# A fused attention and maxout kernel on one core: loads placed where GpSimd has no mark to set, one z loaded a step ahead, PSUM pairs given out by PE's own times

## The chip, the cores and the metric

The kernel runs on one core of a Trainium2 chip. The core has five engines that take part here: TensorE (PE in the profile; PEld is its weight load, which runs beside the matmuls), VectorE (DVE), ScalarE (ACT), GpSimd (POOL) and SyncE (SP). SP does nothing but issue DMAs; POOL issues DMAs too and sets small marks. Two DMA queues carry nearly all data: q0, filled by POOL, and q1, filled by SP. The metric is the device time of one execution in microseconds, lower is better.

## The reference

There are eight sequences of 3072 tokens. For each, attention without a softmax is computed from z (64 wide) and v (256 wide), and gated with u (256 wide). A maxout MLP with 1024 hidden units follows on every token.

```python
# u, v: (8, 3072, 256); z: (8, 3072, 64); w1, w2: (256, 1024); w_out: (1024, 256)
scores = (1.0 / 3072) * np.matmul(z, z.transpose(0, 2, 1))
attn = np.maximum(scores, 0.0) ** 2
x = (u * np.matmul(attn, v)).reshape(8 * 3072, 256)
h1, h2 = x @ w1, x @ w2
out = np.maximum(h1, h2) @ w_out
```

All data come and go as float32; the products are made in bfloat16 with float32 sums in PSUM.

## The kernel before

**Tiles and steps.** The work is cut into 48 steps, n = 6b + s: step s of sequence b makes the outputs of 512 tokens (a group: G = 4 blocks of 128; NG = 6 groups a sequence). In the steady state a step takes about 18.5 us, a sequence 111.2 us. Each step has these stages, and the MLP of a step runs three steps later (LAG = 3), between the products of the later step:

- scores: z zᵀ for pairs of blocks, from zT, the transposed z of the sequence (`score`, L260). ACT or DVE apply the relu and the square (`relu`, `square`) and give a tile `a_sb`. Since the scores are symmetric, blocks that are needed in the other orientation are turned by DMA transposes on SP (`turn`).
- attention products: (attn v)ᵀ. The first three steps (PLAIN) do it plainly. Later steps use a Winograd form of Strassen's method with seven products in place of eight. It needs sums of blocks: DVE makes S1 to S4 from the attention tiles for each step and group, and folds v once for each sequence (`add_fold`, tile `lf`, from the six v tiles of the sequence in pairs of two). On PE the products are four lists a step: Xa, Xb, Ya, Yb, each going over the six groups.
- gating: DVE makes xT from the product in PSUM (`acc`) and uT (L296). uT is u, turned by one DMA transpose on SP.
- MLP: max(h1, h2) is h2 plus the relu of h1 − h2. So d jobs (L1109) multiply x with w1 − w2, ACT or DVE apply the relu and give `g_sb`, and o jobs (L1188) multiply `g_sb` with w_out and x with w2 w_out, which is made once (`W2o_sb`). Copies to `o_sb` and a store by SP follow.

**Half rows and marks.** PE works with 64 of its 128 rows at a time, two matmuls side by side, each for a different PSUM bank (`halved`, L99). Both halves of a sum go into the same bank, and so the second half may begin only when the first is through. That is said by a mark: GpSimd sets one column of `mark_sb` when the newest matmul of the first half is done (`mark`, L94 to 97; the memset is L95), and the first matmul of the second half waits for this memset (`fence`, in `matmul`, L86 to 92). Xb waits so for Xa, Yb's first product for Ya's first, the last Ya for Yb; the d and o jobs have marks of their own (L700 to 705, `halves_of`, `parts`). There are 364 marks in all.

**Loads.** u (256 KB a step), v (six of 256 KB a sequence) and z (384 KB a sequence) are loaded by POOL with `load` (L107, L108). A timed load waits for the newest matmul issued at its place in the program. POOL works in its program's order, so a mark that comes behind a load waits for it, and the other way round. z of every sequence from 1 on goes into the same tile, `z_sb_0`; then SP turns it with two transposes into zT (`make_zT`, L117 to 121), which has two buffers.

**What sets the order.** PE's order is written out by hand (`work`, L1267 on) and becomes the list `pe_order`, with planned starts `pe_at` and a planned start of each step, `starts`. `at_step(b, s, us)` (L1472) gives the first PE job planned at or after `us` microseconds into step s of sequence b. `add_u` (L1478), `add_z` (L1506) and `add_v` (L343) take such a job as the place of their load. Before, u of the next step is loaded 4 us into a step (2 us in sequence 0), z of sequence b at (step 2, 9 us) of sequence b − 1, and at (step 3, 8 us) for sequence 1; its turn is at (3, 12), for sequence 1 at (3, 18).

The orders of ACT, DVE, SP and POOL come from a planner that runs while the program is built: `link` (L1680) draws up who depends on whom, `find_dues` (L1715) gives each job the time at which it is wanted, from `plan`, which adds up PE's costs (L1710), and `find_orders` (L1739) plays the jobs through with planned costs, with `settle` (L1754) for the DMAs. This is repeated for 24 rounds, and the round with the earliest end of PE is kept. PSUM has three pairs of banks for scores and MLP (`mm`); `share_mm` (L1833) gives each user one of them: of the pairs free in PE's order, that which comes free first. Before, it took the time when a pair comes free from the planner's `done`, and it was done again at rounds 2, 4 and 6 (`PAIRS_AT`, L195).

SEVEN (L54), the steps whose output products would use a seven-product form (`add_seven`, L923), is an empty tuple in both kernels.

Of the kernel before, what the change touches and what calls it, by code (L numbers as in the profile page):

```python
# [11 lines left out]
def kernel(  # L12
# [27 lines left out]
    P = 128  # L40
# [142 lines left out]
    ALONE, XB_TO, YA_FROM, YA_FIRST, O_CLEAR = 4, 2, 2, 6, 2  # L183


    PE128, PE256, PE512, SWITCH = 56, 109, 216, 100
    TT = {256: 205, 512: 336, 1024: 603, 1536: 870}
    RELU = {"ACT": 912, "DVE": 1140}
    RELU_LAST = {"ACT": 264, "DVE": 345}
# [2 lines left out]
    LAST_BLOCKS = 60  # L192
    COPY_O = {"ACT": 470, "DVE": 610}
    PATIENCE, WAIT_COST = 400, 20
    ROUNDS, PAIRS_AT = 24, (2, 4, 6)  # L195
    RELU_BIAS, SQUARE_BIAS = 1200, -300
    TURN, TURN_LAG, UT_LAG = 1750, 4000, 7000

# [32 lines left out]
    def tile_of(pool, key):  # L231
        return bufs[pool, key].tile
# [52 lines left out]
    def copy(eng, out_ap, in_ap):  # L285
        pin(nc.scalar.copy(out_ap, in_ap) if eng == "ACT" else nc.vector.tensor_copy(out_ap, in_ap))  # L286
# [609 lines left out]
    def w_half(k, c):  # L896
        return w_out_sb[:, ds(k * KF // 2, KF // 2), ts(c, P)]
# [25 lines left out]
    def add_seven(st):  # L923
# [5 lines left out]
        def R(k, t):  # L929
            return tile_of(*gk)[:, ds(k * KF // 2, KF // 2), ts(t, HW)]  # L930

        def made(i):
            return tile_of(*sk)[:, i]

        halves = [("g", n, 0), ("g", n, 1)], [("g", n, 2), ("g", n, 3)]
        for name, fn, deps in (
# [12 lines left out]
                lag=180,  # L949
            )  # L950

        half_m = range(KF // 2)

        def at_ps(at, j):
            bank, pos, tile_i = at
            return tile_of("mm", ("o", n, tile_i))[:, bank, ds(pos * HW + j * P, P)]

        def run(at, moving_w, x):
            return [(at_ps(at, j), x[:, m, ts(j, P)], moving_w[:, m, :]) for m in half_m for j in range(2)]

        def x_part(at, h, c):
            return [
                (at_ps(at, j), tile_of(*xT)[:, h, dc, ts(j, P)], W2o_sb[:, dc, ts(c, P)])
                for dc in range(KD)
                for j in range(2)
            ]

        def bank_lists():
            return {
                "a": run((0, 0, 0), w_half(0, 0), R(0, 0)) + x_part((0, 1, 0), 0, 0) + run((0, 1, 0), w_half(1, 0), R(1, 0)),
                "b": x_part((1, 0, 0), 1, 0) + x_part((1, 1, 0), 1, 1) + run((1, 0, 0), wf_sb[:, 3], R(1, 1)),
                "c": run((0, 0, 1), wf_sb[:, 2], made(0)) + run((0, 1, 1), wf_sb[:, 1], made(1)),
                "d": run((1, 0, 1), wf_sb[:, 0], R(0, 1)) + x_part((1, 1, 1), 0, 1) + run((1, 1, 1), w_half(1, 1), made(2)),
            }

        def slots(first, end):
            lists = bank_lists()  # L980
            sides = [[(name, i) for name in names for i in range(len(lists[name]))] for names in ("adbc", "bcad")]
            for at in range(first, end):
                for half in range(2):
                    name, i = sides[half][at]
                    second = ("adbc".index(name) > 1) != (half == 1)
                    if second and i == 0:
                        fence.append(marks.pop((n, name)))
                    end_of = i == len(lists[name]) - 1
                    halved(half, *lists[name][i], start=not second and i == 0, stop=second and end_of)
                    if not second and end_of:  # L990
                        marks[n, name] = mark()

        P0, P1 = ("mm", ("o", n, 0)), ("mm", ("o", n, 1))
        base = [("w2o", 0), ("w2o", 1)] + [("wf", i) for i in range(4)]
        firsts = halves[0] + halves[1][:1] + base
        for i, (first, end, deps, new, uses) in enumerate(
            (
                (0, 14, firsts, [P0, P1], [gk, xT]),
                (14, 20, halves[1] + [("G3", n)], None, [gk, xT, sk]),
                (20, 24, [("G1", n)], None, [gk, sk]),  # L1000
                (24, 32, [("G2", n)], None, [gk, xT, sk]),
                (32, 56, [("G4", n)], None, [gk, sk, xT, P0, P1]),
                (56, 72, [], None, [sk, xT, gk, P1]),
            )
        ):
            job(
                ("o", n, i),
                {"PE": (end - first) * PE128},
                lambda _, first=first, end=end: slots(first, end),
                deps=deps,  # L1010
                new=new,
                uses=uses,
                lag=150,
            )

        def ps(i, bank, pos=None):
            t = tile_of("mm", ("o", n, i))[:, bank, :]
# [11 lines left out]
        def right():  # L1029
            return tile_of(*ok).rearrange("p (h j) (c d) -> p h j c d", h=2, c=2)[:, :, :, 1, :]  # L1030

        for name, ways, fn, deps, uses in (
            ("oc0", {"ACT": 270}, lambda e: copy("ACT", C(0, 1), two(ps(0, 0, 0))), [("o", n, 4)], [P0]),
            (
                "oc1",
                {"ACT": 470},
                lambda e: copy("ACT", low(), ps(0, 1).rearrange("p (c j d) -> p c j d", c=2, j=2)),
                [("o", n, 4)],
                [P0],
            ),  # L1040
            ("oA", {"DVE": 336}, lambda e: add(C(0, 0), C(0, 1), two(ps(0, 0, 1))), [("oc0", n)], [P0]),
            ("oB", {"DVE": 336}, lambda e: add(C(0, 1), C(0, 1), two(ps(1, 0, 1))), [("oA", n), ("o", n, 5)], [P1]),
            ("oC", {"DVE": 336}, lambda e: add(two(tile_of(*tk)), C(0, 1), two(ps(1, 0, 0))), [("oB", n)], [P1, tk]),
            ("oD", {"DVE": 603}, lambda e: add(right(), right(), twice(ps(1, 1, 0))), [("oC", n), ("oc1", n)], [P1]),
            ("oE", {"DVE": 336}, lambda e: add(C(0, 1), C(0, 1), two(ps(1, 1, 1))), [("oD", n)], [P1]),
            ("oF", {"DVE": 603}, lambda e: add(low(), low(), twice(tile_of(*tk))), [("oD", n)], [tk]),
        ):
            job(
                (name, n),
                ways,  # L1050
                fn,
                deps=deps,
                new={"oc0": ok, "oC": tk}.get(name),
                uses=[ok] + uses,
                after=[("oc0", n)] if name == "oc1" else (),
                lag=200,
            )
# [221 lines left out]

    def put_o(n, per=2):  # L1280
        if n >= 0 and steps[n].seven:
            for i, count in enumerate((14, 6, 4, 8, 24, 16)):
                put(count * PE128, True, ("o", n, i))
        elif n == last:
            for i in range(G):
                put(1090, True, ("o", n, i))
        elif n >= 0:
            for i, count in enumerate((20, 10, 10)):
                put(count * PE256, True, ("o", n, i))
# [182 lines left out]
    def at_step(b, s, us):  # L1472
        return pe_job_at(starts[NG * b + s] + us * 1000)

    def z_deps(st):
        return [("zT", st.b)] if st.b else []

# [44 lines left out]
    for n in range(len(steps)):  # L1522
        b, s = steps[n].b, steps[n].s
        if n == 0:
            add_u(0, None)
        else:
            pb, ps = divmod(n - 1, NG)
            add_u(n, at_step(pb, ps, 2 if pb == 0 else 4))
    for b in range(1, B):
        if b == 1:  # L1530
            z_at, zT_at = (3, 8), (3, 18)
            v_at = [(4, 8), (4, 13), (4, 17.5), (5, 2), (5, 8), (5, 11)]
        else:
            z_at, zT_at = (2, 9), (3, 12)
            v_at = [(3, 8), (3, 14), (4, 5), (4, 12), (5, 2), (5, 6)]
        add_z(b, at_step(b - 1, *z_at), at_step(b - 1, *zT_at))
        for g, at in zip(v_order(b), v_at):
            add_v(b, g, at_step(b - 1, *at))

    W2, W2T = ("T", "w2"), ("T", "w2T")  # L1540
    bufs[W2] = Buf(lambda tag: widepool.tile([P, KD, Dff], bf16, name="w2_sb", tag=tag))
# [288 lines left out]
        return uses  # L1830


    def share_mm():  # L1833
        def end(key):
            return max([j.done for j in bufs["mm", key].jobs] + [0])

        keys = order["mm"]
        uses = [[], [("mm", keys[0]), ("mm", keys[2])], [("mm", keys[1]), ("mm", keys[3])]]
        free_at = [0, end(keys[2]), end(keys[3])]
        for key, slot in zip(keys, (1, 2, 1, 2)):  # L1840
            bufs["mm", key].slot = slot
        last_use = [-1] * 3
        for key in keys[4:]:
            at = position[taker["mm", key].key]
            slot = min([i for i in range(3) if last_use[i] < at], key=lambda i: free_at[i])
            last_use[slot] = max(position.get(j.key, -1) for j in bufs["mm", key].jobs)
            free_at[slot] = end(key)
            uses[slot].append(("mm", key))
            bufs["mm", key].slot = slot
        return uses  # L1850
# [5 lines left out]
    find_orders()  # L1856
    wide = share_wide()
    pairs = share_mm()
    for turn_no in range(ROUNDS):
        if turn_no in PAIRS_AT:  # L1860
            pairs = share_mm()
        link(wide + pairs)
        find_dues()
        found = find_orders()
# [99 lines left out]
```

## Time and profile before

| | us |
|---|---|
| median of 3 runs | 922.25 (921.33 to 922.66) |
| profiled execution: its own time | 919.85 |
| its span in the trace (granted clock 0.998) | 917.8 |
| PE busy | 904.8 (99%) |
| DVE, ACT, POOL busy | 692.4 (75%), 652.7 (71%), 95.4 (10%) |
| share of 16 DMA engines: q1 (SP), q0 (POOL) | 75.8%, 23.2% |
| u load, v load, z load, issue to landing (medians) | 5.6, 5.7, 6.7 |
| uT transpose, issue to landing (median) | 5.8 |

The span is the time from the first to the last instruction of the profiled execution; 2.05 us of its own time lie around it. "Landing" is the time when the data of a DMA are there, counted from its issue. In rows of the timeline the first number is the start in us, the second the duration, then engine, line, operation and tiles; a bracket at the end gives how long the engine had been idle and what it waited for. A row of the waits reads: engine, its line, who released it; total, number of times, longest. A matmul of 64 rows by 256 columns runs beside that of the other half, and such pairs start every 109 to 110 ns; those with 512 columns every 212 to 216.

### The profile page before, as it was taken

Reading aid. Unit: us, or ns where it says so; the run is one execution under the profiler, and the core shown is the slowest. Engines: PE = TensorE matmul, PEld = TensorE weight load, DVE = VectorE, ACT = ScalarE, POOL = GpSimd, SP = SyncE. Lnnn points to the kernel's source line nnn. Section 1 sums busy time; section 2 is a strip of 40 time slices with the busy share of each in tenths; the row PEclk is TensorE's granted clock in tenths of the full one; section 3 lists DMA queues with packets and bytes.
Section 4 is the critical chain, followed back from the end, with each engine's and each line's share of the span. In section 5 each row is a group of like instructions: output and inputs, shape, how many; then the busy total and the mean of one; then the engine's idle time right before and its main releaser. Section 6 shows DMA issues by size and latency. Waiting matters only on the chain.

```text
span 917.8 us, 31948 instructions
## 1 busy us (share of the span) xinstructions
PE 904.8 (99%) x13813; PEld 668.6 (73%) x13813; DVE 692.4 (75%) x1356; ACT 652.7 (71%) x780; POOL 95.4 (10%) x479
## 2 busy tenths in 40 slices
PE   9998999999999999999999999999999999999998
PEld 3366777777777777777777777778777777777775
DVE  6766788768886888778886788778878777888641
ACT  8865887568766778667786587865888558874534
POOL 2100100111001110011100110001100011000000
PEclk9999999999999999999999999999999999999999
DMA  9999999999999999999999999999999999997711
GB/s 162 122 186 199 177 192 180 161 180 146 172 161 172 182 151 152 172 169 170 152 174 176 156 162 167 166 174 173 161 158 171 145 192 160 168 160 136 115 36 70
DMA packets 382909, 146.32 MB, mean 159 GB/s; under 512 B 361264, under 2 KB 362928, under 8 KB 382768
## 3 DMA queue, kind: packets, MB, share of 16 engines
q1 hardware_dynamic: 366208, 114.54, 75.8%
q0 software_dynamic: 16560, 29.74, 23.2%
q8 instruction: 108, 1.77, 0.8%
q14 instruction: 33, 0.27, 0.1%
HBM read 59.77 MB, written 25.17 MB: 93 GB/s over the span
## 4 chain that ended last, share of the span: by engine, by line
PE 94%; DMA 2%; ACT 2%; issue 1%; POOL 1%; DVE 0%; SPq 0%; POOLq 0%; DVEq 0%
PE acc L87 47%; PE s_ps L87 47%; ACT a_sb L275 1%; DMA uT<-u_sb 1%; DMA zT<-z_sb 1%; ACT a_held L275 0%; POOL z_sb L108 0%; DMA o_sb<-in_z_dram 0%; SPq L104 0%; POOL mark_sb L95 0%; DVE xT L296 0%; ACT a_sb L281 0%; PE tpz L130 0%; DVE a_sb L283 0%; DVE zT L131 0%
## 5 line engine op out<-in xcount | busy, mean ns | idle before, releaser
L87 PEld LDWEIGHTS <-v_sb 64*128 64x128 bf16 (+1 forms) x4464 | 313.5, 94 | 81.4 <-POOL mark_sb L95 16.8
L275 ACT ACTIVATE a_sb<-s_ps 128x1024 bf16<-128x1024 f32 x337 | 302.0, 942 | 62.1 <-PE s_ps L87 59.1
L87 PEld LDWEIGHTS <-lf 64*128 64x128 bf16 x3240 | 251.9, 94 | 45.9 <-POOL mark_sb L95 15.9
L87 PE MATMUL acc<-es,v_sb 64*128 64x256 bf16 x2160 | 277.4, 269 | 0.0
L283 DVE TENSOR_TENSOR a_sb<-a_sb 128x1024 bf16<-128x1024 bf16 (+1 forms) x240 | 149.7, 637 | 145.2 <-ACT a_sb L275 138.7
L87 PE MATMUL acc<-es,lf 64*128 64x256 bf16 x1080 | 247.7, 269 | 0.1
L87 PE MATMUL acc<-a_sb,lf 64*128 64x256 bf16 x1224 | 227.0, 269 | 0.0
L275 ACT ACTIVATE g_sb<-s_ps 128x1024 bf16<-128x1024 f32 x187 | 186.3, 1025 | 13.4 <-PE s_ps L87 12.7
L87 PE MATMUL s_ps<-w_out_sb,g_sb 64*128 64x256 bf16 x3008 | 194.9, 269 | 0.0
L87 PE MATMUL s_ps<-xT,w_sb 64*128 64x512 bf16 (+1 forms) x1484 | 189.8, 377 | 2.9 <-POOL mark_sb L95 2.8
L87 PE MATMUL acc<-aT,lf 64*128 64x256 bf16 x936 | 174.4, 270 | 0.0
L87 PEld LDWEIGHTS <-g_sb 64*128 64x128 bf16 x3008 | 146.3, 94 | 18.2 <-issue 0.4
L286 ACT COPY o_sb<-s_ps 128x512 f32<-128x512 f32 (+1 forms) x98 | 56.5, 577 | 136.7 <-PE s_ps L87 136.7
L289 DVE TENSOR_TENSOR e<-e,acc 128x512 f32<-128x512 f32 (+1 forms) x225 | 126.2, 577 | 29.4 <-ACT e L286 16.2
L87 PE MATMUL acc<-a_sb,v_sb 64*128 64x256 bf16 (+1 forms) x1352 | 140.9, 281 | 1.3 <-POOL mark_sb L95 1.3
L87 PEld LDWEIGHTS <-w_sb 64*128 64x128 bf16 (+1 forms) x1488 | 68.0, 94 | 74.5 <-POOL mark_sb L95 33.7
L87 PE MATMUL s_ps<-zT 64*128 64x512 bf16 (+2 forms) x774 | 115.9, 335 | 3.6 <-DMA zT<-z_sb 3.3
L289 DVE TENSOR_TENSOR es<-aT 128x1536 bf16<-128x1536 bf16 (+1 forms) x117 | 106.6, 930 | 0.2
L95 POOL MEMSET mark_sb<- 128x1 bf16 x364 | 37.1, 102 | 616.6 <-PE s_ps L87 440.5
L281 ACT ACTIVATE a_sb<-a_sb 128x1024 bf16<-128x1024 bf16 (+1 forms) x98 | 93.1, 969 | 1.2
L292 DVE TENSOR_TENSOR es<-a_sb 128x512 bf16<-128x512 bf16 x198 | 80.3, 418 | 15.2 <-PE acc L87 14.7
L87 PE MATMUL acc<-aT,v_sb 64*128 64x256 bf16 x936 | 85.8, 271 | 0.2 <-DVE xT L296 0.2
(58 smaller groups left out, 557.2 us busy)
## 6 DMA issues: line engine op xcount, KB each, us to landing
out_dram<-o_sb SPq DMA_DIRECT2D x47, 512.0 KB, 4.6
v_sb<-in_v_dram POOLq DMA_DIRECT2D x48, 256.0 KB, 5.7
u_sb<-in_u_dram POOLq DMA_DIRECT2D x48, 256.0 KB, 5.6
aT<-a_sb SPq DMA_TRANSPOSE x230, 4.9
z_sb<-in_z_dram POOLq DMA_DIRECT2D x7, 384.0 KB, 6.7
w_sb<-in_moe_w_dram POOLq DMA_DIRECT2D x2, 512.0 KB, 10.9
uT<-u_sb SPq DMA_TRANSPOSE x48, 5.8
a_sb<-a_sb SPq DMA_TRANSPOSE x45, 4.4
```

Source lines behind the costliest of these rows:

```text
L87: newest[0] = pin(nc.tensor.matmul(*args, **kw)).ins
L95: ins = pin(nc.gpsimd.memset(mark_sb, 0.0)).ins
L275: pin(nc.scalar.activation(out_ap, in_ap, AF.Relu))
L281: pin(nc.scalar.activation(ap, ap, AF.Square))
L283: pin(nc.vector.tensor_mul(ap, ap, ap))
L286: pin(nc.scalar.copy(out_ap, in_ap) if eng == "ACT" else nc.vector.tensor_copy(out_ap, in_ap))
L289: pin(nc.vector.tensor_add(*args))
L292: pin(nc.vector.tensor_sub(*args))
```

## The change

It has four parts.

1. A function `quiet` is added. A place planned from the start of step 3 (LAG) on moves on to the next job of a fixed set: the first group's Xb, Ya or Yb of a step. It is applied to all timed loads of u, z and v, not to those of the weights.
2. z of sequence 1 is loaded at (step 2, 6 us) in place of (3, 8), and turned at (3, 2) in place of (3, 18).
3. `share_mm` gives the pairs out once, and takes the time at which a pair comes free from PE's plan: the planned start of the pair's last PE job, that job's PE time, and a constant for the reads behind it (1200 ns; 900 for outputs).
4. `add_seven` is written anew with three PE jobs in place of six, and the constants and `put_o` with it. With SEVEN empty it is not called.

```diff
-    ROUNDS, PAIRS_AT = 24, (2, 4, 6)
+    ROUNDS = 24
+    READ_O, READ_PLAIN = (1500, 3000), (900, 900)
...
+    QUIET = {("Xb", n, st.groups[0]) for n, st in enumerate(steps)} | {
+        (part, n, st.groups[i]) for n, st in enumerate(steps) for part, i in (("Ya", 0), ("Yb", 0))
+    }
+
+    def quiet(at):
+        i = pe_order.index(at[0])
+        if pe_at[i] < starts[LAG]:
+            return at
+        found = [key for key in pe_order[i:] if key in QUIET]
+        return found[:1] or at
...
-            add_u(n, at_step(pb, ps, 2 if pb == 0 else 4))
+            add_u(n, quiet(at_step(pb, ps, 2 if pb == 0 else 4)))
     for b in range(1, B):
         if b == 1:
-            z_at, zT_at = (3, 8), (3, 18)
+            z_at, zT_at = (2, 6), (3, 2)
             v_at = [(4, 8), (4, 13), (4, 17.5), (5, 2), (5, 8), (5, 11)]
...
-        add_z(b, at_step(b - 1, *z_at), at_step(b - 1, *zT_at))
+        add_z(b, quiet(at_step(b - 1, *z_at)), at_step(b - 1, *zT_at))
         for g, at in zip(v_order(b), v_at):
-            add_v(b, g, at_step(b - 1, *at))
+            add_v(b, g, quiet(at_step(b - 1, *at)))
...
     def share_mm():
-        def end(key):
-            return max([j.done for j in bufs["mm", key].jobs] + [0])
-
         keys = order["mm"]
...
-        free_at = [0, end(keys[2]), end(keys[3])]
+        free_at, last_use = [0, 0, 1], [-1] * 3
...
             last_use[slot] = max(position.get(j.key, -1) for j in bufs["mm", key].jobs)
-            free_at[slot] = end(key)
+            user = pe_order[last_use[slot]]
+            reads = 1200
+            if key[0] == "o":
+                reads = (READ_O if steps[key[1]].seven else READ_PLAIN)[key[2] % 2]
+            free_at[slot] = plan[user] + jobs[user].ways["PE"] + reads
...
-    for turn_no in range(ROUNDS):
-        if turn_no in PAIRS_AT:
-            pairs = share_mm()
+    for _ in range(ROUNDS):
         link(wide + pairs)
```

More of the change, by code (lines that the diff above doesn't have):

```diff
@@ L183 @@
     ALONE, XB_TO, YA_FROM, YA_FIRST, O_CLEAR = 4, 2, 2, 6, 2
-    PE128, PE256, PE512, SWITCH = 56, 109, 216, 100
+    PE128, PE256, PE512, SWITCH, CHANGE = 56, 109, 216, 100, 150
     TT = {256: 205, 512: 336, 1024: 603, 1536: 870}
@@ L952, in add_seven, with run @@
         half_m = range(KF // 2)
+        def run(todo, ends=False):
+            for at, moving_w, x in todo:
+                for m in half_m:
+                    for j in range(2):
+                        first = (m, j) == (0, 0) and at[1] == 0
+                        last = (m, j) == (KF // 2 - 1, 1) and ends
+                        matmul(
+                            at_ps(at, j),
+                            x[:, m, ts(j, P)],
+                            moving_w[:, m, :],
+                            start=first,
+                            stop=last,
+                        )
@@ L954, in at_ps @@
         def at_ps(at, j):
-            bank, pos, tile_i = at
+            tile_i, bank, pos = at[2], at[0], at[1]
             return tile_of("mm", ("o", n, tile_i))[:, bank, ds(pos * HW + j * P, P)]
[L958 to L966, printed above, removed]
@@ L971, in bank_lists @@
[L971 to L977, printed above, removed]
@@ L979, in slots @@
[L979 to L991, printed above, removed]
@@ L993, in add_seven, with x_part, first @@
-        P0, P1 = ("mm", ("o", n, 0)), ("mm", ("o", n, 1))
+        def x_part(at, h, c, last):
+            for dc in range(KD):
+                for j in range(2):
+                    matmul(
+                        at_ps(at, j),
+                        tile_of(*xT)[:, h, dc, ts(j, P)],
+                        W2o_sb[:, dc, ts(c, P)],
+                        start=False,
+                        stop=last and dc == KD - 1 and j == 1,
+                    )
+        def first(_):
+            run([((0, 0, 0), w_half(0, 0), R(0, 0)), ((0, 1, 0), w_half(1, 0), R(1, 0))])
+            x_part((0, 1, 0), 0, 0, True)
+            run([((1, 0, 0), wf_sb[:, 3], R(1, 1))])
+            x_part((1, 0, 0), 1, 0, False)
+            x_part((1, 1, 0), 1, 1, True)
@@ L994, in add_seven, with second, third @@
+        def second(_):
+            run([((0, 0, 1), wf_sb[:, 2], made(0)), ((1, 0, 1), wf_sb[:, 0], R(0, 1))])
+        def third(_):
+            run([((0, 1, 1), wf_sb[:, 1], made(1))], ends=True)
+            run([((1, 1, 1), w_half(1, 1), made(2))])
+            x_part((1, 1, 1), 0, 1, True)
         base = [("w2o", 0), ("w2o", 1)] + [("wf", i) for i in range(4)]
-        firsts = halves[0] + halves[1][:1] + base
-        for i, (first, end, deps, new, uses) in enumerate(
-            (
[L998 to L1003, printed above, removed]
-            )
-        ):
[L1006 to L1014, printed above, removed]
+        for i, (fn, ns, deps, new, uses) in enumerate(
+            (
+                (first, 36 * PE128 + CHANGE, halves[0] + halves[1] + base, ("mm", ("o", n, 0)), [gk, xT]),
+                (second, 16 * PE128, [("G3", n), ("G1", n)], ("mm", ("o", n, 1)), [gk, sk]),
+                (third, 20 * PE128, [("G2", n), ("G4", n)], None, [sk, xT, ("mm", ("o", n, 1))]),
+            )
+        ):
+            job(("o", n, i), {"PE": ns}, fn, deps=deps, new=new, uses=uses, lag=150)
@@ L1030, in right @@
             return tile_of(*ok).rearrange("p (h j) (c d) -> p h j c d", h=2, c=2)[:, :, :, 1, :]
+        P0, P1 = ("mm", ("o", n, 0)), ("mm", ("o", n, 1))
         for name, ways, fn, deps, uses in (
-            ("oc0", {"ACT": 270}, lambda e: copy("ACT", C(0, 1), two(ps(0, 0, 0))), [("o", n, 4)], [P0]),
+            ("oc0", {"ACT": 270}, lambda e: copy("ACT", C(0, 1), two(ps(0, 0, 0))), [("o", n, 0)], [P0]),
             (
@@ L1037, in add_seven @@
                 lambda e: copy("ACT", low(), ps(0, 1).rearrange("p (c j d) -> p c j d", c=2, j=2)),
-                [("o", n, 4)],
+                [("o", n, 0)],
                 [P0],
@@ L1041, in add_seven @@
             ("oA", {"DVE": 336}, lambda e: add(C(0, 0), C(0, 1), two(ps(0, 0, 1))), [("oc0", n)], [P0]),
-            ("oB", {"DVE": 336}, lambda e: add(C(0, 1), C(0, 1), two(ps(1, 0, 1))), [("oA", n), ("o", n, 5)], [P1]),
+            ("oB", {"DVE": 336}, lambda e: add(C(0, 1), C(0, 1), two(ps(1, 0, 1))), [("oA", n), ("o", n, 2)], [P1]),
             ("oC", {"DVE": 336}, lambda e: add(two(tile_of(*tk)), C(0, 1), two(ps(1, 0, 0))), [("oB", n)], [P1, tk]),
@@ L1281, in put_o @@
         if n >= 0 and steps[n].seven:
-            for i, count in enumerate((14, 6, 4, 8, 24, 16)):
-                put(count * PE128, True, ("o", n, i))
+            put(36 * PE128 + CHANGE, True, ("o", n, 0))
+            put(16 * PE128, True, ("o", n, 1))
+            put(20 * PE128, True, ("o", n, 2))
         elif n == last:
@@ L1833, in share_mm @@
     def share_mm():
-        def end(key):
-            return max([j.done for j in bufs["mm", key].jobs] + [0])
         keys = order["mm"]
         uses = [[], [("mm", keys[0]), ("mm", keys[2])], [("mm", keys[1]), ("mm", keys[3])]]
-        free_at = [0, end(keys[2]), end(keys[3])]
+        free_at, last_use = [0, 0, 1], [-1] * 3
         for key, slot in zip(keys, (1, 2, 1, 2)):
             bufs["mm", key].slot = slot
-        last_use = [-1] * 3
         for key in keys[4:]:
```

## The prediction

> **What bounds the kernel now.** The busy shares come first: PE is busy 904.8 of 917.8 us (99%), DVE 75%, ACT 71%, POOL 10%. So PE sets the end, and only what makes PE idle or slow can be won. The view of waits says what PE stood still for:
>
> ```profile
> PEld L87 <- POOL mark_sb L95: 66.4, 178, 1.8
> ...
> PEld L87 <- DMA zT<-z_sb: 3.6, 1, 3.6
> PE s_ps L87 <- DMA zT<-z_sb: 3.3, 1, 3.3
> ...
> PE s_ps L87 <- POOL mark_sb L95: 2.8, 6, 0.5
> ...
> PE acc L87 <- POOL mark_sb L95: 1.3, 1, 1.3
> ```
>
> The columns are us in total, times, longest. PEld's 66.4 is no loss, since weight loads run beside matmuls. PE's own rows are: zT once, six waits on a mark in s_ps, one in acc. Next, the timeline at each. One of the six:
>
> ```profile
> 164.35 0.10 POOL L95 MEMSET mark_sb<- 128x1 bf16 x1 [2.75 <-PE s_ps L87]
> ...
> 164.86 0.53 POOL L108 DMA_DIRECT2D z_sb<-in_z_dram  x1 [0.41 <-PE s_ps L87]
> ...
> 165.38 0.12 POOL L95 MEMSET mark_sb<- 128x1 bf16 x1
> ...
> 165.55 1.04 PE L87 MATMUL s_ps<-xT,w_sb 64*128 64x512 bf16 x8 [0.45 <-POOL mark_sb L95]
> ```
>
> The load of z holds POOL for 0.53 us, the mark stands behind it, and PE waits for the mark. The matmuls start at 164.73 and 165.55, 0.82 apart where 0.21 is usual: 0.61 lost. It recurs at 276.76, 387.97, 499.18, 610.39 and 721.89 (0.608 to 0.635). The acc row is a load of u:
>
> ```profile
> 847.74 0.54 POOL L108 DMA_DIRECT2D u_sb<-in_u_dram  x1 [4.98 <-PE s_ps L87]
> 848.27 0.28 POOL L95 MEMSET mark_sb<- 128x1 bf16 x2
> ...
> 848.44 0.39 PE L87 MATMUL acc<-a_sb,v_sb 64*128 64x256 bf16 x4 [1.34 <-POOL mark_sb L95]
> ```
>
> This load began 2.70 us after the matmul it waits for, all others 0.31; its mark came 1.50 us late. Last, the wait for zT of sequence 1, and the windows with the granted clock (second number: PE busy; after POOL's: PEclk):
>
> ```profile
> 84.12 0.39 PE L87 MATMUL s_ps<-zT 64*128 64x256 bf16 x4 [3.30 <-DMA zT<-z_sb]
> ```
> ```profile
> 82.10:85.50 3.40, 1.38 (x20) 0.94 (x22) 1.85 (x4) 0.95 (x1) 0.20 (x2) 0.98 1.22 238
> 85.50:88.90 3.40, 3.40 (x38) 2.46 (x34) 0.69 (x1) 2.05 (x3) 0.00 (x1) 0.52 1.19 199
> ```
>
> PE waits from 80.66 to 84.12 (3.46), then runs a window at clock 0.52, which costs 3.40 x 0.48 = 1.63; by the spacing of the matmuls it is 1.65.
>
> **The change, part by part.** PE's own list of matmuls is the same in both programs; the loads' places, the orders of SP and ACT, DVE's order up to about 130 us, and the PSUM pairs differ.
>
> (a) z of sequence 1, earlier. z goes out at 62.52, lands at 68.00, and SP issues its two zT transposes at 75.06 to 79.33, landing at 84.07. After the change the load waits for the matmul at 46.27, and SP has the transposes ahead of its entries of about 67: at 4.3 us of issue and 4.7 more to land they are there by 77 at the latest, ahead of 80.66. The wait goes, and the slow window with it: −3.46 −1.65 = **−5.1**. What is late next: the inputs that DVE makes for PE stand over 2 us ahead in this stage. On POOL nothing is queued behind the load until 54; u of step 4 takes its old place at 63.7, 2 us ahead of the next mark (65.81), and its turn at 68.87 goes behind zT without harm, since uT stands some 20 us ahead of its xT from here on.
>
> (b) z of sequences 2 to 7 moves from 164.86 to 167.31 (and alike), where the next mark is 0.9 us or more away: 6 x 0.61 = **−3.7**. Its zT is still turned by SP's place in step 3; zT stood 0.18 to 1.69 us ahead of its first score, and SP's new order has it one entry ahead of uT in most sequences, some 1.5 us more. So nothing is late there.
>
> (c) The u load of 847.74 moves to 849.23, behind that mark: **−1.5**.
>
> (d) The other moved loads of u and v. Here a new risk: the u load in step 5 of seven sequences (108.19, 219.38 ... 775.7) ends 0.03 us ahead of the next mark PE needs. In before six v loads have 0.04, and none made PE wait; such a mark costs nothing when free. Two marks (665.37, 781.68) were 0.29 late with no load ahead; whether these go or three come is open: 0, from −0.6 to +0.3.
>
> (e) What z's new place costs. At 46.27 the queues are full: w_out (40.84) and u (41.76) are being read, and SP has issued uT of step 2 at 43.56 to 45.84. While GpSimd's loads (q0) are served, transposes (q1) nearly stand; only after 50.4 do they run:
>
> ```profile
> q0 software_dynamic: 1023, 0.67, 128.2%
> q1 hardware_dynamic: 169, 0.04, 8.5%
> ```
> ```profile
> q1 hardware_dynamic: 4224, 1.05, 128.6%
> ```
>
> The first is 46.5 to 50.0, the second 50.5 to 55.0. uT lands at 52.58, and DVE's xT waits for it already:
>
> ```profile
> 52.67 0.69 DVE L296 SCALAR_TENSOR_TENSOR xT<-acc,uT 128x512 bf16<-128x512 f32 x1 [3.09 <-DMA uT<-u_sb]
> ```
>
> PE then loses 0.39 at 54.62. z's packets began 1.1 us after its issue at the old place (62.52, 63.6); from 47.4 it stands behind u in q0, ahead of the moment (50.4) at which q1 is let in. Its 0.39 MB take 2.1 us at the first row's 0.67 MB in 3.5; at the old place they took up to 3.8 (63.6 to 67.4). I take 2.2, nearest to the crowded row: uT lands at 54.8. DVE's new order puts a square ahead of xT, which would let PE go at 54.02 + 2.2 = 56.2 against 54.23 wanted: 2.0 lost, against 0.39 now: **+1.6** (−0.4 with uT untouched, +3.2 with 3.8).
>
> Does that wait bring a slow window? The nearest row is the 1.50 us stand at 848: the window behind it is at 1.00. The 3.46 stand had one. I take 0, bound +1.7. [...]
>
> (f) DVE's new order in steps 3 to 7: a fold for sequence 1 ends at about 123.3 where its product is wanted at 123.04: **+0.2** (0 to 0.4).
>
> (g) PSUM pairs: almost everywhere pairs 0 and 1 change names; one score at 47.45 waits 0.1 for a relu, within the wait of (e). 0. The rewritten seven-product output is never built (SEVEN is empty): 0.
>
> Sum: −5.1 −3.7 −1.5 +0 +1.6 +0.2 = −8.5. The profiled execution's 919.85 (span 917.8 and 2.05 around it) becomes 911.35. It stands 2.40 below the median of the runs, so I forecast 922.25 − 8.5 = **913.8**.
>
> **The rivals.**
> 1. The same with a slow window behind the wait at 54: +1.65, up to +1.6 more if z takes 3.8: 915.4 to 917.0. For it: 2.0 us lies between a stand without (1.50) and one with (3.46).
> 2. z is served behind uT 2, and delays only the turns that follow. Then the 0.39 goes, and a product at 58.2 waits about 0.9: +0.5 in place of +1.6: 912.7. For it: uT was issued 2.7 us earlier. Against: q1 at 8.5% while q0 is served.
> 3. Marks are still late at the new places: the seven u loads with 0.03 us of room. At the 0.29 of the late marks seen: 7 x 0.3 = +2.1: 915.9. Against: six loads with 0.04 did no harm.
> 4. Slower. The last v loads of sequences 2 to 7 go out later (218.39 for 217.47), behind them u. DVE runs without a gap for 10.9 us from the fold of these v (227.87) to the sums PE wants, with 0.3 to spare. The fold starts 9.5 us after the load is issued in the new program, so a load that lands L us after issue costs L − 9.8 each. At L = 11.8 it is 2.0 x 6 = 12: 925.8. It ends above 924.1 from L = 11.5 on (1.72 x 6 = 10.3). Seen for this load: 7.13 to 10.41; the 10.41 would cost 0.6. Against: second loads of a pair, as u and v are here, landed after 6.27 to 8.37. For it: a load has been late, by 2.4 us, at 847.74. [...]
> 5. The change does not do what it says: zT still late since SP does not reach it, or z is held. Then (a) is lost: 922.25 − 3.4 = 918.9. At 68.87 to 72.3 SP was busy with others' transposes, but zT's order is fixed ahead of them.
>
> **How the numbers follow.** Forecast 0.45; rival 1 0.20; rival 2 0.14; rival 3 0.08; rival 4 0.08; rival 5 0.05. What this kernel's measurement can tell from no change is about 0.2%, 1.84 us: faster is below 920.4, slower above 924.1. Rivals 1, 2, 3 and 5 end faster, with 0.05 of all these near enough to 920.4 to count as the same: faster 0.87, same 0.05, slower 0.08. The range goes from 911.0 (913.8 less the 2.0 to the lower end of (e), the 0.6 of (d) and the 0.2 of (f)) to 918.0 (plus 1.65 for a slow window, 1.6 for z at 3.8, 0.3 of (d), 0.2 of (f): 917.6, rounded up). It leaves out rivals 4 and 5, 0.13.
>
> **What would show it.** In the profile after: no wait of PE for zT; no row of PE s_ps on a mark with 0.5, none of 1.3 in acc; no clock of 0.5 at 85. A wait of DVE for uT near 50 to 55 of 5 us instead of 3.09, and a PE gap of some 2 us at 54 to 56: (e). A slow window behind it is rival 1. Gaps at 108, 219 and on of 0.3 are rival 3; PE waiting on sums about 235, 346 is rival 4. The forecast is wrong if DVE, not the loads, holds PE in steps 2 to 4, where its order changes most, or if a later place of u or v delays what I followed only by before's times.

## The result, and the profile after

The changed kernel takes 913.67 us (median of 9 runs, 910.70 to 917.57), the kernel before 921.33 (9 runs, 917.08 to 923.31). The ratio is 0.993, with a 95% interval of 0.9907 to 0.9952. The forecast was 913.8. Medians here and below are of all runs of a kernel, while the ratios leave out three runs that took over 1.5% longer than the fastest of their kernel. The profiled execution took 915.26, its span is 913.3; the profiled execution of the kernel before took 919.85, 4.6 more.

The rows of PE (and one of DVE) among the waits of the changed kernel; columns as before:

```profile
DVE lf L290 <- DMA v_sb<-in_v_dram: 3.3, 1, 3.3
...
PE acc L87 <- DVE lf L290: 2.7, 1, 2.7
...
PE s_ps L87 <- POOL mark_sb L95: 0.5, 2, 0.3
PE acc L87 <- DMA v_sb<-in_v_dram: 0.5, 1, 0.5
```

PE no longer waits for zT, of its waits for marks 0.5 us is left, and there is a new wait: DVE for a v, and PE for the fold that DVE makes of it. The next rows show the timeline where z of sequence 2 is loaded, and where the load of u stood ahead of a mark near 848:

```profile
165.19 0.10 POOL L95 MEMSET mark_sb<- 128x1 bf16 x1 [0.33 <-PE s_ps L87]
...
166.51 0.10 POOL L95 MEMSET mark_sb<- 128x1 bf16 x1 [1.22 <-PE s_ps L87]
...
167.13 0.53 POOL L108 DMA_DIRECT2D z_sb<-in_z_dram  x1 [0.51 <-PE acc L87]
```
```profile
846.50 0.54 POOL L108 DMA_DIRECT2D u_sb<-in_u_dram  x1 [2.90 <-PE s_ps L87]
847.03 0.28 POOL L95 MEMSET mark_sb<- 128x1 bf16 x2
...
847.20 1.04 PE L87 MATMUL s_ps<-xT,w_sb 64*128 64x512 bf16 x8 [0.32 <-POOL mark_sb L95]
```

The marks come first now and z behind them. The load of u is still ahead of a mark, but of one that is wanted later: PE loses 0.48 instead of 1.50.

PE's order is the same in all kernels here, so one matmul can be followed through every trace. From the start of the 1751st matmul (152.59 us before, 153.00 after) to the end of the span, the kernel before takes 765.20 us, the changed one 760.33. So 4.9 us are won behind 150 us, and the first part, where z's new place should have won 5.1, took 0.4 us longer; together they are the 4.5 us between the spans. The starts of the same matmuls split the 0.4: 4.85 are won near 80 to 90 (the wait for zT and the slow window behind it) and 0.5 near 55; 5.2 are lost between 115 and 131, and 0.55 in the first 10 us, ahead of every load that was moved. That beginning alone differs by some 2 us between the traces of this document. Between 115 and 131 PE stood here; the last two rows are windows with their length, the busy time of PE, PEld, DVE, ACT and POOL, and then the granted clock:

```profile
118.89 0.39 PE L87 MATMUL acc<-a_sb,v_sb 64*128 64x256 bf16 x4 [0.46 <-DMA v_sb<-in_v_dram]
122.02 0.28 PE L87 MATMUL acc<-a_sb,lf 64*128 64x256 bf16 x2 [2.73 <-DVE lf L290]
```
```profile
118.80:122.20 3.40, 0.58 (x8) 0.29 (x10) 0.67 (x2) 0.41 (x1) 0.00 (x0) 1.00 1.30 108
122.20:125.60 3.40, 3.40 (x30) 1.90 (x28) 3.40 (x10) 2.49 (x3) 0.73 (x3) 0.53 1.06 222
```

The v in question was issued at 107.37 and landed 14.1 us later. PE was busy 0.58 us of the first window, and the next one ran at clock 0.53, which costs 3.40 x 0.47 = 1.6.

### The profile page after: what moved, and what is told of

Its sections match the earlier page's. It is cut to its first block, busy times and chain, and to the rows that moved or that the text cites. A ratio compares the mean times of both kernels' runs of the same rounds, so it can differ in the third digit from the quotient of the medians.

```text
span 913.3 us, 31984 instructions
## 1 busy us (share of the span) xinstructions
PE 903.4 (99%) x13813; PEld 667.9 (73%) x13813; DVE 693.3 (76%) x1357; ACT 651.1 (71%) x779; POOL 95.4 (10%) x479
## 4 chain that ended last, share of the span: by engine, by line
PE 96%; DMA 2%; ACT 1%; POOL 0%; issue 0%; DVE 0%; POOLq 0%; DVEq 0%
PE s_ps L87 48%; PE acc L87 48%; DMA v_sb<-in_v_dram 2%; ACT a_sb L276 1%; DMA z_sb<-in_z_dram 1%; ACT a_held L276 0%; PE tpz_c L130 0%; DVE lf L290 0%; POOL u_sb L108 0%; ACT o_sb L287 0%; POOL mark_sb L95 0%; POOL ident masks.py:199 0%; POOL ident masks.py:197 0%; POOL z_sb L174 0%; POOL z_sb L175 0%
## 5 line engine op out<-in xcount | busy, mean ns | idle before, releaser
L276 ACT ACTIVATE a_sb<-s_ps 128x1024 bf16<-128x1024 f32 x337 | 301.9, 942 | 58.2 <-PE s_ps L87 55.9
L87 PEld LDWEIGHTS <-lf 64*128 64x128 bf16 x3240 | 251.8, 94 | 48.6 <-POOL mark_sb L95 15.6
L276 ACT ACTIVATE g_sb<-s_ps 128x1024 bf16<-128x1024 f32 x187 | 185.7, 1025 | 13.7 <-PE s_ps L87 13.3
```

Of the source, the lines that this page charges most:

```text
L87: newest[0] = pin(nc.tensor.matmul(*args, **kw)).ins
L276: pin(nc.scalar.activation(out_ap, in_ap, AF.Relu))
```

## The experiments

My theory was that the parts add up and that the late v was chance of the DMA queues. The rivals were that it belongs to the new order, and that the first part is bound by the amount of DMA work. "First part" below is the time to the 1751st matmul, "rest" what follows. What PE lost at a wait is the distance of two matmul starts beyond the usual one. The runs of one group were made on one chip, beside the kernel before; the second and third group on the same chip.

**First group** (before: 921.4). The changed kernel again; no edit.

> The changed kernel once more, for a second trace and more spans with their clocks. Theory (late v is chance of the DMA queues): the 2.9 us wait of VectorE for a v of sequence 1 near 119 to 122, and the slow window behind it, are in some executions only: spans fall into two groups, about 909 (granted clock 1.000) and 912 to 916 (0.996 to 0.998), and the new trace has either no wait there or one of another length. Rival (the wait belongs to the new order of loads): the second trace has it again at 2.5 us or more, and the spans at clock 1.000 need another cause.

914.1 us, ratio 0.9917 (0.9889 to 0.9945). v took 11.6 us to land in place of 14.1, PE lost 1.10 there and 1.36 at two turns near 102. The wait has another length: it goes with the execution. The two groups of times did not show: the runs at a granted clock of 0.999 to 1.000 took 912.1 to 915.3. The rest is 760.35.

z's place alone:

```diff
-            z_at, zT_at = (3, 8), (3, 18)
+            z_at, zT_at = (2, 6), (3, 2)
```

> The kernel before with z of sequence 1 loaded at (step 2, 6 us) and turned at (3, 2), nothing else. Theory (parts add up): the wait for zT (3.46 us) and the slow window behind it (1.65) go, the six waits of 0.6 and the one of 1.5 at 848 stay: about 5.1 us less than before, ratio 0.9945, and no clock of 0.5 near 85. If the late v of sequence 1 comes with z's new place: 2 to 4 us of it are given back at 119 to 122, ratio 0.997 to 0.999.

919.12 us, ratio 0.9982 (0.9958 to 1.0006). The wait for zT is gone, the six marks and the one near 850 stay, the rest is 765.15. But v took 12.6 us, and PE lost 1.19 and then 3.13 near 120 to 130. The first part took 154.38 us, more than before's 152.59. The 5.1 us of the theory do not come; the ratio is what the second half of the expectation says, that the v gives them back.

Quiet places alone (`QUIET` and `quiet` added, and the three calls):

```diff
-            add_u(n, at_step(pb, ps, 2 if pb == 0 else 4))
+            add_u(n, quiet(at_step(pb, ps, 2 if pb == 0 else 4)))
...
-        add_z(b, at_step(b - 1, *z_at), at_step(b - 1, *zT_at))
+        add_z(b, quiet(at_step(b - 1, *z_at)), at_step(b - 1, *zT_at))
...
-            add_v(b, g, at_step(b - 1, *at))
+            add_v(b, g, quiet(at_step(b - 1, *at)))
```

> The kernel before with the quiet places of loads alone. Theory (parts add up): the six waits for a mark behind the load of z (3.7 us) and the one at 848 (1.5) go, the wait for zT and its slow window (5.1) stay: ratio about 0.9945. Rival (the marks were not what held PE, or the later loads hold it instead): the marks' rows go from the waits of PE, and a wait on v, u or sums of the same size comes: ratio 0.998 or more.

911.68 us, ratio 0.9898 (0.9871 to 0.9926): twice what was expected. The rest is 760.51, 4.7 less than before, as the marks say. The surprise is in the first part: the wait for zT is there, but only 1.20 us long, v landed after 8.1, and PE lost nothing at it. So zT's wait is no fixed 3.46 even where z's place is nearly the old one (63.41, for 62.52).

PSUM's pairs alone (the new `share_mm`, given out once):

> The kernel before with PSUM's pairs given out by PE's plan, nothing else. Theory: the pairs only change names, ratio 1.000, PE's waits as before (zT 3.5, six of 0.6, one of 1.5). Rival (a pair comes free too late somewhere): PE waits for a relu or a copy, 1 us or more, ratio above 1.001.

919.94 us, ratio 0.9984 (0.9962 to 1.0006), the rest 765.22: no difference, as expected. Its trace has zT's wait at 2.04 us, and v after 10.9.

**Second group** (before: 919.04). The changed kernel with z put back:

```diff
-            z_at, zT_at = (2, 6), (3, 2)
+            z_at, zT_at = (3, 8), (3, 18)
```

> The changed kernel with z of sequence 1 put back to (3, 8) and (3, 18). Theory (the first 150 us are bound by DMA: what z's earlier load wins at zT is given back at the v of sequence 1): the time is that of the changed kernel or 1 to 3 us less, near the 911.7 of the quiet places alone; the trace has a wait for zT of 1 to 2 us and none of 1 us or more for v. Rival (the parts add up as forecast): z's place is worth 3 to 5 us, so 917 to 919.

918.41 us (909.75 to 923.37), ratio 0.9988 (0.996 to 1.0016): by its median this is the rival's side, but its profiled execution is the fastest of all profiled ones, 909.75, with no wait for zT and none for v. The rest is 760.30. Neither theory foresees 14 us between executions of one program.

Quiet places and z, the pairs as before (the diff of z above, on the quiet places alone):

> Quiet places and z's new place, the pairs of PSUM given out as before. Theory (z's new place is what costs): as the changed kernel, about 914, with the wait for a v of sequence 1 near 120. Rival (the pairs given out by PE's plan cost what separates 914 from 911.7): 911 to 912, no such wait.

915.31 us, ratio 0.9954 (0.9926 to 0.9983), v after 13.4 us, 2.82 lost. This is what the theory says, but one trace of so variable a wait does not show its cause; see the next run.

Quiet places alone again; no edit.

> The quiet places alone once more, for a second trace and more times. Theory: 911 to 914 again, the steady part (from the 1751st matmul on) 760.5 us as in the first trace, and the first part 149 to 151. If the first 6 runs were lucky: times up to 917 as the changed kernel has.

914.05 us (910.90 to 924.62), ratio 0.995 (0.9922 to 0.9979). The first 6 times were on the low side. In this trace v took 13.7 us instead of 8.1, and PE lost 3.15 at it, while zT was in time. It is the same program, so its order of instructions alone cannot be the cause. The next rows are the DMA queues from the issue of the last v on, 9 us of each trace, first of the first trace of the quiet places, then of the second:

```profile
DMA packets 2603, 2.00 MB, mean 222 GB/s; under 512 B 1992, under 2 KB 1992, under 8 KB 2602
...
q0 software_dynamic: 551, 1.00, 66.0%
q1 hardware_dynamic: 2051, 0.98, 46.2%
```
```profile
DMA packets 1427, 1.24 MB, mean 138 GB/s; under 512 B 1044, under 2 KB 1044, under 8 KB 1426
...
q1 hardware_dynamic: 1097, 0.64, 77.5%
q0 software_dynamic: 329, 0.59, 55.5%
```

Both queues are busy in both, with more than 100% together; in the second trace they move 138 GB/s in place of 222, and 86 GB/s from 109 to 118. The packets took longer: by these rows (share of 16 x 9 us, over the packets) one of q1 took about 32 ns in the first trace and about 102 in the second, one of q0 about 172 and 243. What made them longer is not shown by any run here.

The changed kernel with the v loads of sequence 1 earlier:

```diff
-            v_at = [(4, 8), (4, 13), (4, 17.5), (5, 2), (5, 8), (5, 11)]
+            v_at = [(3, 14), (4, 5), (4, 8), (4, 13), (4, 17.5), (5, 2)]
```

> The changed kernel with the six v loads of sequence 1 issued some 10 us earlier. Theory (their landing is what holds the first part): the wait of VectorE for v near 120 goes, 1 to 3.5 us less than the changed kernel, 911 to 913. Rival (the DMA queues are full whatever the order): another DMA is late instead, a turn, uT or u, and the time stays at 914 or above.

915.56 us, ratio 0.9965 (0.9941 to 0.9988). In its trace v is in time and PE loses nothing at it; a turn costs 0.83 at 101 instead. The times are no better, which is the rival's side.

**Third group** (before: 919.2). The kernel before again, for its trace; no edit.

> The kernel before once more, for a second trace. Theory (what the first trace showed ahead of 130 us was partly that execution's): VectorE does not wait 3 us for uT near 52, SP has issued that uT near 39 in place of 43.6, and the wait for zT near 81 is not 3.46 us but anything from 0 to 3.5; the rest from the 1751st matmul on takes 765.2 us again, with six waits for a mark of 0.6 us and one of 1.5. Rival (the trace was typical): the same waits with the same lengths, within 0.3 us.

920.67 us, one execution. The theory held. The first rows are of its waits; the two others show how SP came to the uT of step 2, first in the first trace of before, then here:

```profile
DVE lf L289 <- DMA v_sb<-in_v_dram: 6.1, 3, 4.7
...
PE s_ps L87 <- POOL mark_sb L95: 2.8, 6, 0.5
...
PE acc L87 <- DVE e L289: 2.4, 1, 2.4
...
PE s_ps L87 <- DMA zT<-z_sb: 1.9, 1, 1.9
...
PE acc L87 <- DVE lf L289: 1.6, 1, 1.6
```
```profile
28.32 11.92 SPq L104 DMA_TRANSPOSE aT<-a_sb  x2
40.34 3.13 SPq L104 DMA_TRANSPOSE w2T_sb<-w_sb  x1
43.56 2.28 SPq L104 DMA_TRANSPOSE uT<-u_sb  x1
```
```profile
32.31 3.01 SPq L104 DMA_TRANSPOSE aT<-a_sb  x1
35.44 3.06 SPq L104 DMA_TRANSPOSE w2T_sb<-w_sb  x1
38.58 1.31 SPq L104 DMA_TRANSPOSE uT<-u_sb  x1
```

The six marks are the same to 0.1 us. All else ahead of 130 us differs: DVE does not wait for uT, zT costs 2.04 and brings no slow window, and the late v costs 1.74 at its fold and 2.54 at a sum (`e`) that DVE makes behind it, which the first trace did not have at all. In the first trace one turn had held SP from 33.01 to 40.24; here it took 3.01.

The changed kernel and the one with z put back, side by side; no new edit.

> The changed kernel a third time, on the same chip and beside the kernel with z put back. Theory (z's new place is worth a little in the mean, since the wait for zT that it takes away is itself there in some executions only): 913 to 915, 1 to 4 us less than with z put back. If z is worth nothing: both at the same time.

> The changed kernel with z of sequence 1 at its old place, beside the changed kernel on one chip. Theory: times spread from 910 to 923, median 915 to 918; the trace has a wait for zT of 0 to 3.5 us near 81. If z is worth what was forecast (3.3 us net): 917. If nothing: the same as the changed kernel.

912.95 us, ratio 0.9944 (0.9917 to 0.9971), and 915.15, ratio 0.9963 (0.9934 to 0.9992). z is worth some 2 us here, with intervals that overlap widely. Granted clocks tell how the times spread: of the changed kernel's 12 runs here, those at 0.999 to 1.000 took 909.4 to 914.5 us, those at 0.994 to 0.996 took 918.4 to 920.7. A window at half clock costs 1.6 us and 0.0018 of the mean, so these last had, by this estimate, two to three such windows.

The changed kernel without the stores of the first four steps:

```diff
-                lambda _: sp_dma(out=out_b[:, ds(c * G, G), :], in_=tile_of(*ok)),
+                lambda _: n < 4 or sp_dma(out=out_b[:, ds(c * G, G), :], in_=tile_of(*ok)),
```

> The changed kernel without the stores of the first four steps (2 MB of output are not written), nothing else. Theory (the first 150 us are bound by the DMA queues, and the late v is theirs): the v loads of sequence 1 land within 9 us, the wait near 120 goes, the times draw together at 909 to 912. Rival (v is late for another reason, the place of the loads or DVE): v takes 11 to 14 us as before, 914.

916.66 us, ratio 0.9973 (0.9938 to 1.0007), and v took 15.6 us, 5.06 lost. In the first trace of the changed kernel three of the four stores are issued ahead of the landing of the late v, at 88.78, 94.71 and 104.21. Without them v was later, not earlier, and the median is not below the 912.95 of the changed kernel beside it. That speaks against the stored bytes as the cause, with one trace; the rest of the DMA work was not varied. The expectation's rival, the place of the loads or DVE, is not shown either.

This trace has a second wait, at 59, when no store would have been issued yet, so it is not the edit's. The first row is the first trace of the changed kernel, the others are this one:

```profile
57.21 0.42 DVE L293 TENSOR_TENSOR es<-aT 128x512 bf16<-128x512 bf16 x1 [0.80 <-DMA aT<-a_sb]
```
```profile
58.99 0.28 PE L87 MATMUL acc<-aT,lf 64*128 64x256 bf16 x2 [1.41 <-DMA aT<-a_sb]
59.05 0.43 DVE L293 TENSOR_TENSOR es<-aT 128x512 bf16<-128x512 bf16 x1 [3.39 <-DMA aT<-a_sb]
...
59.70 0.52 PE L87 MATMUL acc<-a_sb,v_sb 64*128 64x256 bf16 x3 [0.33 <-DMA a_sb<-a_sb]
```
```profile
56.40:59.80 3.40, 1.66 (x27) 1.11 (x25) 0.72 (x2) 0.29 (x1) 0.00 (x0) 1.00 1.39 144
59.80:63.20 3.40, 3.40 (x34) 3.00 (x33) 2.25 (x6) 0.00 (x0) 0.20 (x2) 0.50 1.23 130
```

A turned attention block is late. In all seven traces with z's new place DVE waits for it near 57 to 59, by 0.80 to 3.39 us, and in none of the seven without. PE loses nothing by it in four of them, 0.2 and 0.4 in two, and here 2.2 and a slow window, 3.7 together.

All traces together (us; L is the time from issue to landing of the last v of sequence 1, the next column what PE lost between 115 and 131 to v and to what DVE makes behind it, without slow windows):

| kernel | wait for zT near 81 | L | lost at v | first part | rest |
|---|---|---|---|---|---|
| before | 3.46 | 6.6 | 0 | 152.59 | 765.20 |
| before, again | 2.04 | 13.2 | 4.28 | 153.36 | 765.17 |
| pairs alone | 2.04 | 10.9 | 2.02 | 151.29 | 765.22 |
| z alone | 0 | 12.6 | 4.33 | 154.38 | 765.15 |
| quiet places alone | 1.20 | 8.1 | 0 | 149.25 | 760.51 |
| the same, again | 0 | 13.7 | 3.15 | 151.43 | 760.96 |
| quiet places and pairs | 0 | 8.0 | 0 | 147.53 | 760.30 |
| the same, again | 1.16 | 10.1 | 0 | 148.86 | 760.28 |
| quiet places and z | 0 | 13.4 | 2.82 | 152.50 | 760.26 |
| changed | 0 | 14.1 | 3.51 | 153.00 | 760.33 |
| changed, again | 0 | 11.6 | 1.10 | 151.55 | 760.35 |
| changed, third | 0 | 9.5 | 0 | 148.68 | 760.33 |
| changed, v early | 0 | 6.8 | 0 | 149.14 | 760.96 |
| changed, no stores | 0 | 15.6 | 5.06 | 158.29 | 760.19 |

The rest has two values, with quiet places and without, 4.9 us apart. Both traces of 760.96 have a wait of 0.65 for a later zT, and so has the one without stores. The first part spreads over 11 us. With quiet places what PE loses at v follows L: up to 10.1 v costs nothing, beyond it about L − 10.5.

## Why the prediction was right, point by point

The total came out within its range and near its value. For the quiet places, (b) to (d), the reason is the forecast one: −5.2 forecast, −4.9 measured. For the first part it is luck: (a), (e) and (f) add up to −3.3, the medians leave −2.8 for it, and none of the three keeps its size in the later traces.

- **(b), right.** The six waits behind z's load are gone, 3.77 us measured for 3.7 forecast, in each of the ten traces with quiet places and in none of the four without. That nothing is late behind them is not quite so: in three of the ten a zT of a later sequence held PE for 0.65, once each.
- **(c), mis-sized.** The load of u near 848 still delays a mark: 0.48 is lost where nothing was forecast, so the term is −1.0 for −1.5. The load itself is late again (846.50, with POOL idle for 2.90 us ahead of it); why was not settled.
- **(d), right.** The two late marks (0.61) are gone, two others are late (0.38 at 85.59, 0.28 at 312.63). The seven loads with 0.03 us of room cost nothing, so rival 3 falls. In the rest (b), (c) and (d) make 3.8 + 1.0 + 0.3; the span ends 0.3 later behind the last matmul, so they account for 4.8 of the 4.9.
- **(a), right in mechanism, mis-sized.** In all seven traces with z's new place the wait is gone. But the 3.46 and the slow window were one execution's: in the second trace of before and with the pairs alone it is 2.04. With quiet places, where z goes ahead of u of step 4, it is 1.20, 1.16, 0 and 0 even at z's old place. There, by these four traces, the term is worth 0 to 1.2, not 5.1.
- **(e), the step that failed.** z did stand in full queues, as forecast: it took 9.2 to 12.2 us to land in place of 5.5 to 6.9. (At the old place its packets began 1.3 us after the issue, at 63.82, not 1.1.) But uT of step 2 was in no danger. It was issued at 37.9 to 40.3 in all other traces and landed after 3.1 to 3.5 us, ahead of z's issue. Only the one profiled execution of before had it at 43.56 and 9.0. Forecast +1.6; measured −0.4 against the first trace, which is the lower bound that (e) gave for an untouched uT, and 0 against the second, where the 0.39 is not there either. What came instead is the mechanism of rival 2: uT 2 is ahead of z, and the turn behind is late. Its price of 0.9 at 58.2 was too high for six of the seven traces (0 to 0.4) and too low for one (3.7). Rival 1's wait at 54 never came, but a slow window did follow the turn's wait in that one trace.
- **(f), mis-sized.** 0.2 was forecast from DVE's order, with v in time. With v in time it cost nothing. The fold did hold PE, by up to 5.1 us, because v lands late in some executions. This is rival 4's mechanism, with a formula of the same form (L − 9.8 forecast, about L − 10.5 found), but in sequence 1, which that rival left out. In sequences 2 to 7, where it was placed, v took at most 9.3 us in the changed kernel's traces, and nothing was lost.
- **(g), right.** The pairs alone move nothing that shows.

So of 7.7 us between the medians, 4.9 are shown to be the quiet places. The other 2.8 are left to the first part, and their cause is not shown. z's place is worth between −1 and 2 of them: the three comparisons on one chip say 0.9982 of before (0.9958 to 1.0006), 912.95 against 915.15, and 915.31 against 914.05. Taken together, the runs with quiet places on the chip of the second and third group have a median of 916.1 with z at the old place (36 runs) and 914.4 with z early (24, of the quiet places with z and of the changed kernel). With z's early load a turn is late, by 0.80 to 3.39 us in seven of seven traces; whether it makes v late more often stays open. So does what slows the DMA engines. No version tried beats the changed kernel beyond its spread.

## What to carry to other kernels

The wait that recurred with the same length in sequences 2 to 7 was a property of the program, here the same to 0.1 us in both traces of before: the six of them (0.608 to 0.635 us) could be priced from one trace to a tenth of a microsecond. A wait that occurs once, in the phase where DMA queues are full, may be a draw, as the wait for zT was (3.46 us in one trace of before, 2.04 in the other): take a second trace, or a near relative's, before pricing it. A load on the queue that also sets marks belongs behind the marks that are wanted next: here that took away 3.77 us of waits behind z's load.

## What the runs showed of the hardware

With both queues' shares above 100% together (112.2% and 133.0%), the DMA engines moved 222 GB/s in one execution and 138 in another of the same program, in the 9 us from the issue of the same load, with loads and transposes in flight at once.

Three slow windows, at clock 0.53, 0.52 and 0.50, followed windows in which PE was busy 0.58, 1.38 and 1.66 of 3.40 us; none of these three was empty. Stands of 2.04 and 2.54 us in the second trace of before brought none (its mean granted clock is 1.000), so no length of a stand from which the clock drops is shown.
